# A fused recurrent attention and feed-forward kernel: the column of log w by one product, u by SyncE, the first sums of Y reordered, the decay mask on ScalarE

## The chip, the cores and the metric

One Trainium2 chip, one of its cores. TensorE (PE in the profile), VectorE (DVE), ScalarE (ACT), GpSimd (POOL) and SyncE (SP) run beside each other and wait for each other by semaphores; 16 DMA engines move data between HBM and SBUF. Products land in PSUM, which has 8 banks. The metric is the device time of one execution in microseconds, median of the runs.

## The reference

Two stages. First a recurrence for each of 4 x 8 heads over 768 steps, with a 48 x 48 state that decays by w:

```python
B, H, S, D = r.shape                       # 4, 8, 768, 48
for t in range(S):
    kt, vt, rt = (k[:, :, t].copy(), v[:, :, t].copy(), r[:, :, t].copy())
    cur = np.einsum('bhd,bhe->bhde', u[None] * kt, vt)
    y[:, :, t] = np.einsum('bhd,bhde->bhe', rt, state + cur)
    state = w[None, :, :, None] * state + np.einsum('bhd,bhe->bhde', kt, vt)
```

Then y, as x of 3072 x 384, goes through a feed-forward layer with the square of a ReLU:

```python
h = np.maximum(x @ w_in, 0.0)              # w_in 384 x 2048
return (h * h @ w_out)                     # w_out 2048 x 384
```

## The kernel before

The 768 steps of each batch are cut into 6 chunks of 128; a chunk of one batch with all 8 heads is a *unit*, 24 in all. Units 0 to 3, the first two chunks of batches 0 and 1, are handled as two *pairs* (q = 0, 1): a load of r, k or v fetches 256 steps, and partition p holds steps 2p and 2p + 1. Inside a unit the recurrence becomes matrix products. With the factors w^(t-128) and w^(127-t) (`Wt`, `Wk`, exponentials of multiples of log w, L295 and L299), r and k are scaled (`rh` L341, `kh` L338), transposed (by PE in the first units, `TR`, `TK` L365 and `T` L399; later by the DMA, `XB` L405), and multiplied with each other (`Ap` L385, `A` L412). A mask makes the product strictly causal (`Bp` L393, `Bm` L420), and the masked matrix times v gives Y (`YE` L458, `YD` L438, `Y` L482). The chunks before add rT times the state S0W (`YI` L469, `Y` L480). The state takes k times v (`UP` L492, `U` L502) and a decay mask `WLm` that holds w^128 on the blocks of the diagonal (`S0` L516, `ts` L519, `S` L522). The step's own term is a row sum of r k u (`P0` L344, `P1` L348, `du` L351) times v (`dv` L356): in the pairs PE adds it to Y by a product with the identity (L450, L429), later it is added when Y is copied to bf16 (`xs` L513; L252 on ACT and L254 on DVE are the helper `copy`).

That x is transposed (`X` L527 on PE with the copy `xTc`, later `xX` L534 by the DMA), and enters the feed-forward stage: `F1` (L543; `FA` L555 for the first columns of group 0, one unit at a time) gives hidden blocks of 128 x 512, in groups of two units; `re` (L565 on ACT, L567 on DVE) and `sq` (L572, L574) make the squared ReLU; `F2` (L583) multiplies by w_out into a PSUM bank, `os` copies it out, and `out` (L634, L636) stores it. `V` (L332) and `W` (L335) load quarters of w_in and w_out on POOL's queue, cast to bf16 on the way.

The order is written out by hand. `ORDER` (L25 to L112) is a list of steps `name.indices:engine/slots`, issued from first to last (L645 to L656): `Bp.0.1.1:D/0` is the mask of pair 0, half 1, head parity 1, on DVE, into buffer 0 of its pool. Engines are A (ACT), D (DVE), G (POOL), P (PE), S (SyncE, loads and stores). A PE step's slots are PSUM banks. Each engine runs its own steps in the order of the list, and a wait holds up everything behind it on that engine.

The head of the list, which the change touches most: `w` and `u` (L258, L261) load w and u as one row each. `lw` (L267) takes the logarithm of the w row. `bw` and `bu` (L270, L273) spread the rows over 128 partitions by a product with ones, and `ub` copies u's to SBUF. `bc` (L304) needs log w as a column, one partition for each of the 2 x 48 entries of a head pair, and gets it with eight products of 1 x 128 by 1 x 1 (four, of two passes each); `WLcol` (L310) makes w^128 of it, and `WLm` (L315) spreads that into the mask. `Z` (L615) are products of the identity with itself that nobody reads. `lp` loads the pairs (L326), `ld` the later units (L322).

DVE's order in the head is rh.1, kh.0, P0.0, rh.0, kh.1, rh.3, rh.2, kh.2, kh.3, P1.1, du.0, du.1, the masks Bp.0.1.1, Bp.0.0.1, Bp.0.1.0, Bp.0.0.0, S0.0, ts.1, Bp.1.0.1, xTc.0, Bp.1.0.0, S0.2, ts.3, du.2, re.0.6, du.3. POOL's, behind P1.0 and V.2, is dv.0, dv.1, WLm, P0.2, P1.2, P0.3, P1.3, dv.2, dv.3, W.1, rh.5, W.2, W.3, W.0. PE's is Z.8, bw, bc, bu, TR.0, TK.0, TR.1, Z.2, Ap.0.1, Ap.0.0, TK.1, UP.0, YE.0.1, Z.7, YE.0.0, Ap.1.0, YI.1, UP.1, X.0, X.1, FA.0.0.

Of the kernel before, what the change touches and what calls it, by code (L numbers as in the profile page):

```python
# [30 lines left out]
vb.3:A/2 WLm:G Z.7:P/7 vb.2:A/3 Bp.0.0.0:D/3 YE.0.0:P/2/0 Ap.1.0:P/7/3 P0.2:G/2 S0.0:D ld.v.4:S/4 P1.2:G ts.1:D/1
xs.0:A/0 YI.1:P Bp.1.0.1:D/4 UP.1:P/4/6 X.0:P/5 xs.1:A/1 xTc.0:D/3 Bp.1.0.0:D/6 S0.2:D X.1:P/2 FA.0.0:P/0/3 ts.3:D/0
xTc.1:A/3 FA.0.1:P/0/3 P0.3:G/3 P1.3:G du.2:D/2 re.0.6:D/0 F1.0.0:P/5 dv.2:G du.3:D/3 dv.3:G Wt.2:A re.0.0:A/1 W.1:G
ld.v.5:S/5 Wk.2:A F1.0.1:P/4 Ap.1.1:P/0/2 Bp.1.1.1:D/5 F1.0.2:P/7 re.0.1:A/2 F1.0.3:P/5 rh.5:G/4 re.0.7:A/3
Bp.1.1.0:D/7 YD.1:P/1/2 YI.3:P sq.0.7:A/0 re.0.3:A/4 W.2:G xs.3:D/2 xs.2:A/3 kh.4:D/5 re.0.2:A/5 ld.k.6:S/6 W.3:G
F1.0.4:P/6 X.2:P/4 X.3:P/2 xTc.3:A/0 sq.0.0:A/2 xTc.2:D/0 sq.0.1:D/1 rh.4:D/5 F1.0.5:P/5 W.0:G re.0.4:D/3 sq.0.6:A/3
re.0.5:A/2 P0.4:D/4 F1.1.4:P/1 T.4:P/0 Tc.4:D/4 F1.1.7:P/4 sq.0.5:D/4 F1.1.5:P/5 re.1.4:D/1 re.1.7:A/0 ld.r.6:S/6
sq.0.4:A/5 F1.1.1:P/0 re.1.5:D/2 re.1.1:A/3 sq.1.5:D/6 sq.0.3:D/7 F1.1.0:P/6 kh.5:D/4 F1.1.2:P/4 sq.1.1:A/8 F1.1.6:P/5
re.1.2:A/2 re.1.0:D/4 T.5:P/0 re.1.6:D/3 F2.0.2:P/4 F1.1.3:P/6 ld.r.7:S/7 Tc.5:A/5 P1.4:D du.4:D/4 sq.0.2:D/9
A.4:P/5/0 A.5:P/1/2 sq.1.6:A/10 re.1.3:A/5 sq.1.3:A/11 F2.0.1:P/4 sq.1.0:A/12 F2.0.3:P/4 vb.4:G/4 Bm.4.1:D/0  # L40
Bm.4.0:D/1 sq.1.7:A/13 P0.5:D/1 Bm.5.1:D/2 sq.1.4:A/14 F2.1.1:P/5 Bm.5.0:D/3 F2.1.2:P/5 ld.k.7:S/7 dv.4:G Y.4:P/0
P1.5:G du.5:D/0 F2.3.2:P/6 sq.1.2:A/15 ld.v.7:S/6 ld.k.9:S/0 xs.4:D/4 F2.0.0:P/4 vb.5:A/5 Y.5:P/0 dv.5:D xs.5:D/0
F2.3.0:P/6 P0.6:G/0 P1.6:G ld.v.6:S/7 F2.3.1:P/6 os.0:D/0 ld.r.9:S/0 X.4:P/0 xTc.4:D/1 U.4:P/4 F2.1.0:P/5 X.5:P/0
F2.1.3:P/5 S0.4:D xTc.5:D/1 rh.7:G/6 F1.2.0:P/4 os.1:D/1 F1.2.4:P/0 P0.7:G/2 re.2.0:D/3 out.1:S F1.2.2:P/5 kh.7:D/6
re.2.4:A/5 kh.6:G/0 F1.2.6:P/4 re.2.6:A/4 ld.r.8:S/1 vb.6:A/6 re.2.2:A/0 XB.7:S/6 rh.6:D/0 F1.2.3:P/0 F2.3.3:P/6
kh.9:D/1 re.2.3:A/1 P1.7:D XB.6:S/1 F2.2.2:P/4 os.3:D/2 F1.2.1:P/5 du.7:D/1 S.1:D ld.k.8:S/1 U.5:P/0 S0.5:D dv.7:G
U.6:P/6 re.2.1:A/2 sq.2.1:A/16 F2.2.3:P/4 ld.r.11:S/2 ts.6:D/1 F2.2.1:P/4 sq.2.3:D/17 P0.9:G/3 sq.2.0:A/18 ld.r.10:S/3
F2.2.0:P/4 sq.2.6:A/19 F1.2.7:P/0 os.2:D/3 du.6:D/2 A.7:P/5/6 A.6:P/1/2 ld.k.11:S/2 re.2.7:A/2 vb.7:G/7 F1.2.5:P/4
Bm.7.1:D/0 sq.2.2:A/20 rh.8:G/2 F2.4.0:P/0 ld.k.10:S/3 Bm.7.0:D/1 Bm.6.0:D/2 Bm.6.1:D/3 sq.2.7:A/21 rh.9:G/1 S.3:G
F2.4.1:P/0 re.2.5:D/1 ld.v.8:S/0 XB.9:S/0 P1.9:D dv.6:G out.2:S F2.4.3:P/0 rh.11:G/3 F2.5.0:P/6 ld.v.9:S/1 sq.2.4:A/22  # L50
Y.6:P/5 rh.10:G/5 ld.r.13:S/5 sq.2.5:A/23 F2.5.3:P/6 xs.6:D/1 Y.7:P/4 X.6:P/5 kh.8:G/2 F2.5.1:P/6 xs.7:D/2 P0.8:D/4
xTc.6:A/2 X.7:P/4 U.7:P/5 kh.10:G/5 F2.4.2:P/0 xTc.7:A/2 ts.7:D/0 kh.11:D/3 XB.11:S/2 vb.8:A/0 F1.3.1:P/4 os.4:A/4
S.7:D F1.3.7:P/5 re.3.1:A/3 P0.10:D/1 du.9:D/3 XB.8:S/3 U.8:P/0 F2.5.2:P/6 re.3.7:A/4 vb.9:G/1 S.6:D F1.3.3:P/4
os.5:A/5 XB.10:S/4 P1.8:D re.3.3:D/0 F1.3.4:P/5 F1.3.0:P/6 re.3.4:A/2 rh.13:D/4 ld.k.13:S/4 F1.3.2:P/3 ts.8:D/0
ld.v.11:S/2 re.3.0:A/5 sq.3.1:D/24 U.9:P/5 ld.v.10:S/3 F1.3.5:P/7 re.3.2:A/1 ts.9:D/1 sq.3.0:A/25 sq.3.3:D/26
A.11:P/1/2 A.9:P/6/4 P0.11:D/2 P1.11:G sq.3.2:A/27 F2.6.0:P/5 ld.r.12:S/4 Bm.9.1:D/2 re.3.5:A/3 F2.6.1:P/5 sq.3.7:A/5
Bm.9.0:D/3 ld.v.12:S/4 dv.9:G sq.3.5:A/7 Bm.11.1:D/5 F1.3.6:P/4 Bm.11.0:D/7 sq.3.4:A/3 du.8:D/4 kh.13:G/4 A.10:P/3/7
A.8:P/0/6 re.3.6:A/5 F2.7.0:P/2 Bm.8.0:D/0 sq.3.6:A/9 ld.k.12:S/5 ld.r.15:S/7 Y.9:P/1 vb.11:A/2 F2.7.2:P/2 Bm.8.1:D/1
dv.8:D S.9:G vb.10:A/3 ld.k.14:S/7 F2.6.3:P/5 out.4:A P1.10:G Y.8:P/4 xs.9:D/3 F2.7.3:P/2 xs.8:D/4 P0.13:G/0 X.9:P/0
Bm.10.1:D/4 X.8:P/6 F2.6.2:P/5 xTc.8:A/0 du.11:D/0 xTc.9:D/0 rh.12:G/0 Y.11:P/1 U.10:P/4 du.10:D/2 dv.10:G out.0:S  # L60
# [5 lines left out]
P0.15:G/2 sq.4.3:A/6 F1.5.2:P/4 P1.12:D re.5.7:A/1 ld.k.19:S/3 F2.9.2:P/0 re.4.0:A/4 P1.15:G sq.4.7:A/14 U.11:P/7
sq.4.1:D/10 F2.9.1:P/0 re.5.0:A/5 ld.k.21:S/2 F2.9.3:P/0 sq.5.0:A/13 ts.11:D/1 S.11:G F1.5.5:P/1 re.5.2:A/3 P1.14:D
F1.5.3:P/6 out.7:A ld.r.16:S/1 ts.12:D/0 re.5.5:D/0 sq.4.0:A/11 F1.5.6:P/7 kh.14:G/2 os.6:A/7 F2.8.2:P/4 vb.13:A/5
re.5.6:D/2 dv.13:G F2.9.0:P/0 XB.14:S/0 sq.5.6:A/15 du.12:D/3 A.13:P/2/1 sq.5.5:A/8 A.12:P/5/7 re.5.1:D/5 F2.8.1:P/4
sq.5.7:A/12 XB.15:S/6 Bm.12.0:D/2 P0.17:G/1 sq.5.2:A/16 F2.8.3:P/4 Bm.12.1:D/3 re.5.3:A/4 F2.8.0:P/4 ld.v.14:S/7  # L70
# [617 lines left out]
```

## Time and profile before

| what | value |
|---|---|
| median of 3 runs | 169.44 us (169.03 to 169.59) |
| the profiled execution | 170.19 us |
| its span, first to last instruction | 168.5 us |
| granted clock, core 0 | 1.000 |
| HBM read, written | 20.45 MB, 4.72 MB |

The busiest groups, as instructions x mean: L583 on PE 368 x 326 ns, L543 on PE 612 x 264 ns, L572 on ACT 70 x 626 ns, L565 on ACT 67 x 595 ns, L420 on DVE 40 x 681 ns. Means are from start to modelled end; matmuls overlap, so the distance from one start to the next is shorter.

How to read the rows: a row in order of time is "start us, us, engine line operation out<-in shape xcount [idle before <-what ended it]". Rows of the same line are merged, so that the second number of a row with x4 covers four instructions from the first start to the last end; consecutive instructions of one engine overlap by some 0.1 us. "SPq" and "ACTq" are the issuing of a DMA. A row of the chain of waits is "start, us, what": the chain that ended last, traced back. A row by stretches gives, for each engine, busy us and the number of instructions, then the granted clock, the share of the 16 DMA engines' time and GB/s; the share can pass 1 as packets overlap.

### The profile page before, as it was taken

The page shows a single profiled execution, that of the slowest core. Times are in us where ns is not written, and L with a number is a line of the kernel's source. Part 1 is how long each engine was busy: PE and PEld are TensorE (multiplying, and loading weights), DVE is VectorE, ACT ScalarE, POOL GpSimd, SP SyncE. Part 2 cuts the span into 40 slices and gives each one's busy share as a digit, 9 for nine tenths or more (in the row PEclk, how much of TensorE's full clock was granted, in tenths as well). Part 3 has the DMA queues.
Part 4 walks back from the last instruction along what each step waited for, and adds up shares of the span by engine and source line. Part 5 has one row for each costly group of instructions (what it writes and reads, how often), then busy time and mean ns, then how long its engine had stood idle before and what let it go on. Part 6 is the DMA issues. An engine that isn't in the chain of part 4 may idle for free.

```text
span 168.5 us, 4507 instructions
## 1 busy us (share of the span) xinstructions
PE 161.8 (96%) x1778; PEld 122.4 (73%) x1778; DVE 134.3 (80%) x253; ACT 101.4 (60%) x189; POOL 100.5 (60%) x125
## 2 busy tenths in 40 slices
PE   4999999899999999999999999999999999999993
PEld 1686888568766867788766888666887666898762
DVE  5689979987999979989897969998878965955400
ACT  4687697831772697349782469941298492254731
POOL 6779781248399218995999797599536660300000
PEclk9999999999999999999999999999999999999999
DMA  5999999979999799999999999995879931320032
GB/s 131 321 236 193 196 150 215 205 141 205 150 180 197 154 204 211 202 192 200 191 204 139 220 227 220 174 199 135 162 163 130 267 86 24 108 83 0 2 142 95
DMA packets 97785, 28.02 MB, mean 166 GB/s; under 512 B 92530, under 2 KB 97524, under 8 KB 97764
## 3 DMA queue, kind: packets, MB, share of 16 engines
q1 hardware_dynamic: 93872, 22.42, 67.6%
q0 software_dynamic: 3008, 4.13, 12.8%
q10 hardware_dynamic: 884, 1.18, 2.2%
q8 instruction: 14, 0.23, 0.6%
q14 instruction: 7, 0.06, 0.1%
HBM read 20.45 MB, written 4.72 MB: 149 GB/s over the span
## 4 chain that ended last, share of the span: by engine, by line
PE 63%; DMA 16%; DVE 7%; POOL 6%; issue 4%; SPq 3%; ACT 0%; POOLq 0%
PE bank L583 28%; PE bank L543 26%; DMA W<-in_moe_w_out_dram 6%; DMA ldk<-in_k_dram 3%; DMA ldr<-in_r_dram 2%; DMA xT<-xs 2%; PE bank L482 2%; DMA rkT<-rk 2%; SPq L326 2%; PE bank L412 2%; DVE Bm L420 2%; PE bank L480 2%; PE bank L597 2%; POOL dv L356 1%; POOL P L348 1%
## 5 line engine op out<-in xcount | busy, mean ns | idle before, releaser
L583 PE MATMUL bank<-W,hq 128*128 128x384 bf16 x368 | 68.7, 326 | 0.6 <-DMA W<-in_moe_w_out_dram 0.4
L543 PE MATMUL bank<-xT,W 128*128 128x256 bf16 (+1 forms) x612 | 68.6, 264 | 0.2 <-DMA xT<-xs 0.2
L565 ACT ACTIVATE hr<-bank 128x512 bf16<-128x512 f32 x67 | 38.9, 595 | 37.6 <-PE bank L543 33.6
L543 PEld LDWEIGHTS <-W 128*128 128x128 bf16 x612 | 54.7, 98 | 8.8 <-DMA xT<-xs 0.6
L583 PEld LDWEIGHTS <-hq 128*128 128x128 bf16 x368 | 33.9, 98 | 19.3 <-issue 0.7
L572 ACT ACTIVATE hq<-hr 128x512 bf16<-128x512 bf16 x70 | 40.9, 626 | 4.6 <-DVE hr L567 4.1
L420 DVE TENSOR_TENSOR Bm<-bank,maskJT 128x512 bf16<-128x512 f32 x40 | 25.5, 681 | 3.2 <-PE bank L412 3.1
L567 DVE TENSOR_SCALAR hr<-bank 128x512 bf16<-128x512 f32 x29 | 19.6, 684 | 7.0 <-PE bank L543 4.9
L356 POOL TENSOR_TENSOR dv<-ldv,du 128x384 f32<-128x384 f32 (+1 forms) x18 | 15.9, 891 | 11.5 <-DVE du L351 8.2
L348 POOL TENSOR_TENSOR P<-P,ub 128x384 f32<-128x384 f32 x15 | 15.9, 1062 | 11.2 <-DVE P L344 10.8
L344 POOL TENSOR_TENSOR P<-ldr,ldk 128x384 f32<-128x384 f32 x13 | 13.7, 1054 | 4.7 <-DMA ldr<-in_r_dram 3.4
L341 POOL TENSOR_TENSOR rk<-ldr,Wt 128x384 bf16<-128x384 f32 x15 | 16.5, 1105 | 0.0
L574 DVE TENSOR_TENSOR hq<-hr 128x512 bf16<-128x512 bf16 x26 | 13.3, 523 | 2.1 <-ACT hr L565 1.9
L338 POOL TENSOR_TENSOR rk<-ldk,Wk 128x384 bf16<-128x384 f32 x12 | 12.6, 1055 | 2.6 <-DMA ldk<-in_k_dram 2.6
L513 DVE TENSOR_TENSOR xs<-bank,dv 128x384 bf16<-128x384 f32 x20 | 11.0, 552 | 2.6 <-PE bank L482 1.1
L351 DVE TENSOR_REDUCE du<-P 128x8 f32<-128x384 f32 x24 | 12.8, 542 | 0.0
L522 POOL TENSOR_TENSOR S0W<-ts,WLm 128x384 bf16<-128x384 f32 x10 | 10.3, 1032 | 1.5 <-DVE ts L519 1.5
L254 DVE COPY os<-bank 128x384 f32<-128x384 f32 x11 | 6.0, 550 | 6.2 <-PE bank L583 6.1
L519 DVE TENSOR_TENSOR ts<-bank,S0W 128x384 f32<-128x384 f32 x16 | 8.8, 550 | 2.1 <-PE bank L502 1.1
L482 PE MATMUL bank<-vb,Bm 128*128 128x48 bf16 x160 | 9.5, 183 | 0.0
L252 ACT COPY os<-bank 128x384 f32<-128x384 f32 (+2 forms) x14 | 6.3, 460 | 4.5 <-PE bank L583 2.5
L254 POOL CAST vb<-ldv 128x384 bf16<-128x384 f32 x10 | 5.6, 564 | 5.7 <-DMA ldv<-in_v_dram 5.7
(87 smaller groups left out, 173.4 us busy)
## 6 DMA issues: line engine op xcount, KB each, us to landing
ldr<-in_r_dram SPq DMA_DIRECT2D x20, 192.0 KB, 3.8
ldk<-in_k_dram SPq DMA_DIRECT2D x20, 192.0 KB, 4.1
ldv<-in_v_dram SPq DMA_DIRECT2D x20, 192.0 KB, 3.5
out_dram<-os SPq DMA_DIRECT2D x9, 192.0 KB, 2.4
W<-in_moe_w_in_dram POOLq DMA_DIRECT2D x4, 384.0 KB, 9.2
W<-in_moe_w_out_dram POOLq DMA_DIRECT2D x4, 384.0 KB, 8.5
...
```

The costliest lines, as they stand in the source:

```text
L341: e.tensor_mul(rk[slot[f"rk{i}"]][:, 0, :, 0:D], loaded("r", i), Do.factor("t", i % 2 if i < PAIRED else 2))
L344: e.tensor_mul(P0b[slot[f"P{i}"]], loaded("r", i), loaded("k", i))
L348: e.tensor_mul(t, t, bank("bu")[:, 0 : H * D].rearrange("p (h d) -> p h d", h=H) if i in EARLY_U else ub)
L356: e.tensor_mul(dv_of(i) if i < PAIRED else dvb[slot[f"dv{i}"]], loaded("v", i), t)
L420: e.tensor_mul(Bmb[slot[f"Bm{i}{h}"]], heads(bank(f"bA{i}{h}"), 128), mask_b)
L482: e.matmul(y[:, hc, D * h : D * (h + 1)], m[h][:, hc, :], vb[:, 2 * hc + h, :], start=(c == 0), stop=True, skip_group_check=True,)
L543: e.matmul(hp[:, fi, :], W1[f // 4][:, c, 256 * (f // 2 % 2) : 256 * (f // 2 % 2 + 1)].rearrange("p (m j) -> p j m", j=2)[:, f % 2, :], xt ...
L565: e.activation(hr, hp, AF.Relu)
L567: e.tensor_scalar_max(hr, hp, 0.0)
L572: e.activation(hq, hr, AF.Square)
L574: e.tensor_mul(hq, hr, hr)
L583: e.matmul(bank(f"bO{i}")[:, 0:d_model], hqb[slot[f"hq{g},{f // m}"]][:, at : at + L], W2[q][:, f % 4, :], start=(seen[i] == 1 and f % 4 = ...
```

## The change

- **bc.** `w4` (on ACT's queue, where u was) loads w as 4 partitions of 2 x 48; `l4` (ACT) takes its logarithm into a zeroed 4 x 2 x 64 tile; `bc` is one product of that tile with a 4 x 4 identity, and stands behind TK.0 on PE instead of between bw and bu.
- **u** is loaded by SyncE, behind the first r and ahead of the first k.
- **YE.** The four products with dv come behind the last products of YE.0.0, not ahead of those of YE.0.1; the first product of each bank opens it (start), all others add. Ap.1.0 goes ahead of YE.0.0.
- **WLm** goes from POOL to ACT, between RC.1 and KC.1; WLcol from between the factors to behind KC.0.
- **Z.2 and Z.7** are gone. Two small DVE steps (zeroing of the tile, the 4 x 4 identity) are added at the start.
- **DVE's head** becomes rh.1, rh.0, kh.0, kh.1, P0.0, rh.3, rh.2, P1.1, du.1, kh.2, kh.3, du.0, the masks; re.0.6 goes to ACT.
- **POOL's head:** dv.1 ahead of dv.0; w_out's quarters in the order W.2, W.1, rh.5, W.3, W.0.
- **Later:** sq.0.2 ahead of P1.4 (DVE); F1.2.5 ahead of A.7; A.9 ahead of A.11; U.10 from behind Y.11 to ahead of X.9; F2.19.0 and Y.22 ahead of F1.10.2 (all PE); P1.9 (unit 9's product with u) from ahead of xs.6 to behind xs.7; xTc.9 ahead of du.11 (DVE); out.14 from SyncE to POOL, out.12 earlier on POOL. Some 40 steps get other PSUM banks.

```diff
-w:A mP.0:G mP.1:G lp.r.0:S/0 lp.k.0:S/0 tab:A lw:A Z.8:P/0 bw:P/1 lp.r.1:S/1 lp.v.0:S/0 mJ:G u:A lp.k.1:S/1 Wt.1:A/2
-lp.v.1:S/1 bc:P/3 P0.1:G/0 Wk.0:A/4 rh.1:D/0 ld.r.5:S/4 Wt.0:A/5 bu:P/6 kh.0:D/1 V.3:G WLcol:A P0.0:D/1 Wk.1:A/7
...
+w:A mP.0:G mP.1:G lp.r.0:S/0 u:S lp.k.0:S/0 tab:A lw:A Z.8:P/0 w4:A bw:P/1 lp.r.1:S/1 lp.v.0:S/0 mJ:G lp.k.1:S/1
+bu:P/6 Wt.1:A/2 lp.v.1:S/1 Wt.0:A/5 rh.1:D/0 P0.1:G/0 Wk.0:A/4 rh.0:D/1 Wk.1:A/7 ld.r.5:S/4 kh.0:D/1 V.3:G kh.1:D/0
+ub:A l4:A TR.0:P/0 P0.0:D/1 V.0:G ld.k.4:S/4 RC.0:A/0 TK.0:P/3 rh.3:D/2 rh.2:D/3 V.1:G P1.1:D du.1:D/1 bc:P/6 TR.1:P/2
+KC.1:A/3 vb.3:A/2 Ap.1.0:P/6/0 vb.2:A/3 Bp.0.0.0:D/3 YE.0.0:P/5/3 P0.2:G/2 S0.0:D ld.v.4:S/4 P1.2:G ts.1:D/1 xs.0:A/0
...
+    w4t = const.tile([HP, 2, D], FP32, name="w4")
+    l4t = const.tile([HP, 2, 64], FP32, name="l4")
+    eye4 = const.tile([HP, HP], FP32, name="eye4")
...
+    nc.vector.memset(l4t, 0.0)
...
+    nc.vector.tensor_copy(eye4, identity[0:HP, 0:HP])
...
+        def w4(e):
+            e.dma_start(out=w4t, in_=w.rearrange("(a b) d -> a b d", b=2))
+
+        def l4(e):
+            e.activation(l4t[:, :, 0:D], w4t, AF.Ln)
+
         def bc(e):
-
-            for hc in range(HP):
-                e.matmul(
-                    bank("bc")[:, hc : hc + 1], pair(lrow.rearrange("p (o a) b -> p o a b", o=1), 0, hc), ones[:, 0:1],
-                    start=True, stop=True, skip_group_check=True,
-                )
+            e.matmul(bank("bc")[:, 0:HP], l4t.rearrange("p a b -> p (a b)"), eye4, start=True, stop=True)
...
-                e.tensor_copy(
-                    WLm[64 * h : 64 * h + D, :, D * h : D * (h + 1)],
+                copy(
+                    e, WLm[64 * h : 64 * h + D, :, D * h : D * (h + 1)],
...
         def YE(e, q, h):
             y = [heads(bank(f"bY{2 * q + x}"), 2 * D) for x in range(2)]
-            if h:
-                for a in range(2):
-                    for x in range(2):
-                        e.matmul(
-                            y[x][Do.half(a)], identity[Do.half(x), Do.half(x)],
-                            dv_of(2 * q + a)[Do.half(x)].rearrange("p (a e) d -> p a (e d)", e=2),
-                            start=True, stop=False, skip_group_check=True,
-                        )
             for hc in range(HP):
...
+                            start=(h == 1 and hc == 0 and a == 0), stop=(a == 1 and h == 1), skip_group_check=True,
+                        )
+            if h == 0:
+                for a in range(2):
+                    for x in range(2):
+                        e.matmul(
+                            y[x][Do.half(a)], identity[Do.half(x), Do.half(x)],
+                            dv_of(2 * q + a)[Do.half(x)].rearrange("p (a e) d -> p a (e d)", e=2),
                             start=False, stop=True, skip_group_check=True,
                         )
```

More of the change, by code (lines that the diff above doesn't have):

```diff
@@ L31 @@
[L31 to L60, printed above, removed]
@@ L66 @@
[L66 to L70, printed above, removed]
@@ L103 @@
+F2.18.1:P/6 Bm.22.0:D/7 F2.18.3:P/6 Bm.22.1:D/5 F2.18.0:P/6 F2.19.0:P/3 Y.22:P/4 F1.10.2:P/2 re.10.2:D/3 F1.10.0:P/0
+xs.22:D/2 Bm.23.1:D/6 xX.22:S/0 F1.10.1:P/1 os.18:D/2 F1.10.5:P/5 re.10.0:D/2 out.18:G F1.10.3:P/2 re.10.5:D/5
 Y.23:P/4 sq.10.5:D/22 F2.19.2:P/3 xs.23:D/3 re.10.3:A/4 sq.10.3:A/23 xX.23:S/1 sq.10.2:A/0 F1.11.1:P/7 out.17:G
```

107 lines of the change are left out of this document (69 added, 38 removed).

## The prediction, as it was put on record

> **What bounds the kernel now.** I read first the busy shares of the page and the busy time by stretches, then the chain of waits up to 45 us, then the order in time of PE, DVE, POOL, ACT and SyncE up to 36 us, and at last PE's few gaps after that. In each fence rows of one view stand in order of time, with others between them left out.
>
> ```profile
> PE 161.8 (96%) x1778; PEld 122.4 (73%) x1778; DVE 134.3 (80%) x253; ACT 101.4 (60%) x189; POOL 100.5 (60%) x125
> ...
> 20.60:24.00 3.40, 3.40 (x66) 2.73 (x64) 2.29 (x7) 3.08 (x7) 3.38 (x6) 1.00 0.86 129
> 24.00:33.00 9.00, 8.43 (x89) 6.60 (x88) 8.77 (x18) 7.23 (x13) 1.95 (x3) 1.00 1.16 205
> ...
> 32.90 2.11 PE L583 MATMUL bank<-W,hq 128*128 128x384 bf16 x12 [0.43 <-DMA W<-in_moe_w_out_dram]
> ```
>
> PE is busy for 96% of the span, and its feed-forward products cannot be had for less. So the time is the moment at which they begin, plus their sum, plus the gaps. What can be gained lies before 16.63 us, where the first of them starts (below), and in the gaps, of which that at 32.90 is the largest. The DMA engines (the share ahead of the GB/s) are full from 24 to 33 us, at 1.16, and less so in the stretch before, at 0.86.
>
> What sets 16.63? Rows of DVE, of PE and of ACT:
>
> ```profile
> 9.61 1.02 DVE L338 TENSOR_TENSOR rk<-ldk,bank 128x384 bf16<-128x384 f32 x2 [0.75 <-DMA ldk<-in_k_dram]
> 10.54 0.55 DVE L348 TENSOR_TENSOR P<-P,ub 128x384 f32<-128x384 f32 x1
> 11.01 1.00 DVE L351 TENSOR_REDUCE du<-P 128x8 f32<-128x384 f32 x2
> 11.94 2.47 DVE L393 TENSOR_TENSOR Bm<-bank,maskP 128x512 bf16<-128x512 f32 x4
> ...
> 7.81 2.74 PE L365 MATMUL bank<-identity,rk 128*128 128x128 bf16 x24
> 13.15 0.51 PE L450 MATMUL bank<-dv,identity 64*64 64x384 bf16 x4
> 15.39 0.51 PE L492 MATMUL bank<-vb,rk 64*128 64x96 bf16 x16
> 15.84 0.53 PE L527 MATMUL bank<-identity,xs 128*128 128x128 bf16 x6
> 16.63 1.50 PE L555 MATMUL bank<-xT,W 128*128 128x128 bf16 x24 [0.26 <-DVE xT L254]
> ...
> 14.87 1.10 ACT L252 CAST xs<-bank 128x384 bf16<-128x384 f32 x2 [0.22 <-PE bank L458]
> ```
>
> DVE is done with rh.3 and rh.2 at 8.86, waits 0.75 for the second k load, which lands at 9.59 (chain row below), and then runs without a pause: kh.2, kh.3, P1.1, du.0, du.1 and four masks Bp, until 14.41. Behind the last mask come YE.0.0, the copy xs.0 (14.87), the transposes X (15.84, behind UP.1 at 15.39), the copy to xT and the first feed-forward product (16.63).
>
> **The change part by part.**
>
> *DVE's order in the head.* P1.1 and du.1 move ahead of kh.2, into the wait for k. They cost 11.01 - 10.54 = 0.47 and (11.94 - 11.01) / 2 = 0.46, and can start when the DVE pipeline takes the next one, near 8.79: du.1 lasts until 9.72. kh.2 then starts at 9.72 instead of 9.61, with kh.3, du.0 and the first mask behind it: that mask moves by 0.11 - 0.93 = -0.82, from 11.94 to 11.12. P1.1 needs the broadcast u by 8.79:
>
> ```profile
> 4.68 1.70 PE L304 MATMUL bank<-ones,lrow 1*128 1x1 f32 x8
> 6.25 1.62 PE L273 MATMUL bank<-urow,ones 1*128 1x384 f32 x2
> ...
> 2.29 0.23 ACTq L261 DMA_DIRECT2D urow<-in_u_dram  x1
> 6.42 0.17 ACT L310 ACTIVATE wcol<-bank 128x4 f32<-128x4 f32 x1
> 7.91 0.48 ACT L252 COPY ub<-bank 128x384 f32<-128x384 f32 x1 [0.87 <-PE bank L273]
> ```
>
> *One product for the column of log w.* The eight small products (6.25 - 4.68 = 1.57 of PE) leave the way, so bu can start at 4.68 and end near 6.3; the copy ub (0.48), behind the four factors on ACT, is done near 7.3, 1.5 ahead of need. So u may land as late as 6 without a loss. The transposes TR.0 start when rh.0 is done, now second instead of fourth on DVE, near 6.6 instead of 7.81, and RC.0, KC.0 and the products Ap come earlier with them; the masks wait for DVE, not for these. The new product with two passes costs some 2 x 1.70/8 = 0.43 behind TK.0, where PE waits for rh.2 anyway. If l4 were late, TR.1 and Ap would queue behind it; it is about as small as L310 (0.17), and its load goes out where u's did, 5 us before. RC.0, KC.0 and the casts of v stand behind l4 on ACT and have those 1.2 us to give.
>
> *u on SyncE.* One more issue ahead of k.0. It took 0.23 on ACT; here it delays every load behind it by 0 (if the DMA engines set the pace) to 0.28 (that and the step):
>
> ```profile
> 0.81 0.46 SPq L326 DMA_DIRECT2D ldr<-in_r_dram  x1
> 1.94 1.10 SPq L326 DMA_DIRECT2D ldr<-in_r_dram  x1
> 4.28 5.31 DMA ldk<-in_k_dram
> ```
>
> The third issue takes 1.10 where the first of the same size took 0.46: the queue is full by then, and the pace is not that of issuing. I take 0; with kh.2 at 9.72 the first 0.11 of a delay is free anyhow, which leaves 0.17 for the range.
>
> *Y of pair 0.* YE.0.1 no longer waits for dv; the four products with dv (13.15 to the next at 13.60, 0.45) come behind YE.0.0 instead. So xs.0 gains only 0.82 - 0.45 = 0.37 and starts near 14.5. That doesn't bind: X.0 waited for UP.1 until 15.84, half a microsecond after xs.0 was done (14.87 + 0.48 = 15.35). With YE done near 14.5, YI.1, UP.1 (0.45 to X.0) and xs.0 all end near 15.05, and the first feed-forward product comes near 15.88: **-0.75**. Z.2 and Z.7, products that feed nothing, go too.
>
> *The decay mask on ACT.* It leaves POOL (0.74 below) and stands on ACT ahead of KC.1 and the casts of v.2 and v.3. KC.1 waits for TK.1, so for kh.3, until about 12; RC.1 is done near 11.5. Two copies of at most 0.37 end at 12.2 at the latest. A push of 0.2 on KC.1 would pass to Ap.1.0 and Bp.1.0, which are wanted from 14.6 on and have over 1 us. I take 0.
>
> ```profile
> 18.14 0.54 DVE L351 TENSOR_REDUCE du<-P 128x8 f32<-128x384 f32 x1
> ...
> 13.22 0.74 POOL L315 COPY WLm<-wcol 48x192 f32<-48x192 f32 x2
> 19.83 0.83 POOL L356 TENSOR_TENSOR dv<-ldv,du 128x384 bf16<-128x384 f32 x1 [0.23 <-DVE du L351]
> 21.38 1.01 POOL L341 TENSOR_TENSOR rk<-ldr,Wt 128x384 bf16<-128x384 f32 x1
> 22.33 2.19 POOL L335 DMA_DIRECT2D W<-in_moe_w_out_dram  x3
> ...
> 23.08 9.77 DMA W<-in_moe_w_out_dram
> ```
>
> With the mask off POOL, dv.2 and dv.3 wait for DVE alone: du.2 comes at 18.14 - 0.75 = 17.4, du.3 right behind it since re.0.6 goes to ACT (idle there), and two times 0.83 from 17.95 on end at 19.6 instead of 20.66. So the issues of w_out come about 1.05 earlier. W.2, wanted first, goes first; W.3, whose landing at 32.85 ends the gap at 32.90, is issued from 22.0 instead of 23.08. The transfers start where the DMA engines had room (0.86). Bounds for its landing: unmoved, which leaves PE at 32.90; or 1.05 and more earlier (rh.5, 1.01, no longer parts the first two), and then PE gains its 0.75 and the gap, 1.18 in all. I take **-0.8 to -1.05** there.
>
> *Past 34 us.* What is left of that must pass one spot, where DVE runs without a pause from the landing of r.13 to xs.9 and xs.8, and PE waits for those:
>
> ```profile
> 38.68 0.97 SPq L322 DMA_DIRECT2D ldr<-in_r_dram  x1
> 40.44 1.19 SPq L634 DMA_DIRECT2D out_dram<-os  x2
> 55.88 4.05 DMA ldr<-in_r_dram
> 59.95 0.56 DVE L341 TENSOR_TENSOR rk<-ldr,Wt 128x384 bf16<-128x384 f32 x1 [0.87 <-DMA ldr<-in_r_dram]
> 67.26 1.01 DVE L513 TENSOR_TENSOR xs<-bank,dv 128x384 bf16<-128x384 f32 x2
> 69.68 0.17 PE bank L502 x4
> ```
>
> r.13 is issued in an almost unbroken row of SyncE steps that starts at 40.44 with out.1, which waits for a copy that PE drives; SyncE is idle from 39.65 to 40.44. So that row, and DVE's with it, can start **0.8** earlier even if no load before it does. I carry -0.8. At this spot U.10 (0.17) moves ahead of X.9 into PE's wait: **-0.17**. The swap of A.9 and A.11, F1.2.5 ahead of A.7, and P1.9 (unit 9's product with u) behind xs.6 and xs.7 fill gaps ahead of this spot, so they count 0. Other bank numbers, dv.1 ahead of dv.0, out.14 and out.12 on POOL: 0, since the trace has PE waiting for no bank; a bank that comes free late would cost at most the copy that frees it, 0.5 to 0.7.
>
> *The end.*
>
> ```profile
> 139.34 2.12 PE L583 MATMUL bank<-W,hq 128*128 128x384 bf16 x12
> 141.71 0.83 PE L543 MATMUL bank<-xT,W 128*128 128x256 bf16 x6 [0.25 <-DMA xT<-xs]
> 143.56 0.65 PE bank L583 x4
> 142.65 0.69 DVE L567 TENSOR_SCALAR hr<-bank 128x512 bf16<-128x512 f32 x1 [1.55 <-PE bank L543]
> ```
>
> Twelve products at 0.65 per four end at 141.30; the next starts at 141.71, so 0.41 is lost. F2.19.0 (0.65) and Y.22 now lie in that wait. But on DVE re.10.2 (142.65) still stands ahead of xs.22 and gets its product later, so unit 22's transpose may come up to 0.45 later. Between 0 and -0.41 I take **-0.25**.
>
> **Sum:** -0.8 - 0.17 - 0.25 = -1.22. The profiled execution took 170.19 (its span 168.5 and 1.7 around it), so 168.97 by its own time; the median of the runs shown is 169.44, 0.75 less, which gives **168.2**.
>
> **The rivals.**
>
> *A: the loads hold it.* If r.13 lands when it does now, DVE's run and PE behind 67.9 stay where they are; only -0.17 - 0.25 = -0.4 is left: 169.0. For it: the share of 1.16 up to 33 us. Against: SyncE's idle 0.79.
>
> *B: PE stays at half rate for longer; slower than before.* Twenty-four products of 128 columns take 2.74 us from 7.81 on and 1.50 from 16.63 on. The PEclk row shows nothing of it. The slow ones still run here:
>
> ```profile
> 11.86 0.92 PE L365 MATMUL bank<-identity,rk 128*128 128x128 bf16 x8
> ```
>
> So PE reaches its full rate only after nearly unbroken work from 7.81 to 12.78, 5.0 us. The change takes Z.2, Z.7 and eight products out. If the waits between the masks now break the run, the count starts anew at 15.88, half rate lasts until 20.9 and costs 2.5: 169.44 - 1.22 + 2.5 = 170.7. It decides from a switch at 15.88 + 2 x 1.22 = 18.3 on. Against it: TR.0 to UP.0 is about as dense as before, 1 us earlier (6.6 to 12.4). The Trainium skill, "TensorE: Matmul & The Clock Gate", section "Part 1: The HAM clock gate", says that the clock is halved until a free-running window of about 3.4 us has been busy. By that rule, an estimate, a first busy window that ends by 15.9 costs nothing, and one that ends at 19.3 costs 1.7 and gives 169.9. The trace agrees that the rate doubles late; where the window stands, no run here shows.
>
> *C: all of it comes through.* PE 1.18 early behind 32.9, the loads follow, the end gives 0.41: -1.18 - 0.17 - 0.41 = -1.76, 167.7.
>
> *D: the change doesn't do all it says in the head*, since u, the masks on ACT or the dv products push xs. Half of the 0.8 is left: 168.6, within the forecast's own range.
>
> **How the numbers follow.** Forecast with D 0.54 (167.9 to 168.9), A 0.22 (168.8 to 169.4), B 0.14 (169.5 to 170.8), C 0.10 (167.3 to 167.9). The range of 167.4 to 169.8 leaves out most of B and the edge of C. A measurement of this kernel can tell 0.3%, 0.5 us, from no change: faster is below 168.93, slower above 169.95. Faster: 0.51 + 0.10 + a third of A = 0.68; slower: most of B, 0.11; same: 0.21.
>
> **What would show it.** Right: the first mask on DVE at 11.1, the first feed-forward product at 15.9, W.3 landed by 32.1 with PE's gap there no longer than 0.4, r.13 at 59.1, xs.8 by 67.5, no wait of F1 for xT near 140. Wrong: P1.1 waiting for ub, or k.1 landing past 9.72; 128 columns still at 0.11 us behind 15.9; r.13 still at 59.9; a new wait for a bank.

## The result and the profile after

The change made the kernel slower: 171.63 us against 168.94 us, ratio 1.0131 (95% interval 1.0082 to 1.0181); in a second set, beside other runs, 1.0073 (1.0034 to 1.0111). The forecast was 168.2 us, range 167.4 to 169.8. Times are medians of all executions, while ratios compare undisturbed executions only, on both sides: of the runs below, e11 lost half of its executions to that, and e18's profiled one ran at a mean granted clock of 0.58, so that only its times are used.

The profiled execution took 171.94 us, span 170.2; the one before 170.19 and 168.5. The last product starts 1.75 later (167.16 instead of 165.41), as the whole time. Busy shares of the page after, which hardly move:

```profile
PE 162.9 (96%) x1766; PEld 122.5 (72%) x1766; DVE 134.7 (79%) x254; ACT 102.3 (60%) x193; POOL 99.8 (59%) x124
```

The head after, in order of time, SyncE's issues, POOL and DVE:

```profile
1.32 0.46 SPq L266 DMA_DIRECT2D urow<-in_u_dram  x1
...
6.83 1.00 POOL L350 TENSOR_TENSOR P<-ldr,ldk 128x384 f32<-128x384 f32 x1 [2.47 <-DMA ldk<-in_k_dram]
7.79 2.49 POOL L338 DMA_DIRECT2D W<-in_moe_w_in_dram  x3
...
6.79 1.02 DVE L344 TENSOR_TENSOR rk<-ldk,bank 128x384 bf16<-128x384 f32 x2 [0.25 <-DMA ldk<-in_k_dram]
9.12 0.71 DVE L354 TENSOR_TENSOR P<-P,ub 128x384 f32<-128x384 f32 x1
10.40 1.02 DVE L344 TENSOR_TENSOR rk<-ldk,bank 128x384 bf16<-128x384 f32 x2
11.81 2.47 DVE L399 TENSOR_TENSOR Bm<-bank,maskP 128x512 bf16<-128x512 f32 x4
```

k.0 lands at 6.69 (5.45 before). DVE waits 0.25 for it and POOL 2.47, so that the loads of w_in go out at 7.79 instead of 6.53. P1.1 starts 0.33 later than forecast (9.12, not 8.79) and takes 0.71 instead of 0.55 (to the start of the next one 0.74, forecast 0.47), k.1 lands at 10.38 (9.59 before), and the first mask comes at 11.81: of the forecast 0.82, 0.13 is left.

PE after, in order of time:

```profile
15.68 0.82 PE L498 MATMUL bank<-vb,rk 64*128 64x96 bf16 x16
16.43 0.82 PE L533 MATMUL bank<-identity,xs 128*128 128x128 bf16 x6
...
17.38 2.33 PE L561 MATMUL bank<-xT,W 128*128 128x128 bf16 x24
...
32.98 2.83 PE L589 MATMUL bank<-W,hq 128*128 128x384 bf16 x16
...
37.99 0.37 PE L488 MATMUL bank<-vb,Bm 128*128 128x48 bf16 x8 [0.67 <-DVE xs L519]
...
58.49 0.81 PE L549 MATMUL bank<-xT,W 128*128 128x256 bf16 x6 [0.45 <-DVE ts L525]
...
141.33 2.77 PE L589 MATMUL bank<-W,hq 128*128 128x384 bf16 x16
```

FA starts 0.75 later (16.63 before) and its 24 products take 2.33 instead of 1.50: until 19.15 they run at half rate. The gap at 32.9 is gone, as forecast: W.3 lands at 31.99, and its four products start at 33.65 inside the row at 32.98, 0.75 later than before only because PE comes later. Two waits are new, before Y.5 (37.99) and in F1.3 (58.49). From one start to the next, less the columns, they cost 0.83 and 0.61. The gap of 0.41 near 141 is gone, as forecast (F2.19.0 is part of the row at 141.33), but (below) other executions without the change lack it too.

POOL after, and the longest piece of the chain of waits:

```profile
21.08 1.48 POOL L341 DMA_DIRECT2D W<-in_moe_w_out_dram  x2
22.57 1.02 POOL L347 TENSOR_TENSOR rk<-ldr,Wt 128x384 bf16<-128x384 f32 x1
23.52 1.48 POOL L341 DMA_DIRECT2D W<-in_moe_w_out_dram  x2
34.46 0.67 POOL L259 CAST vb<-ldv 128x384 bf16<-128x384 f32 x1 [9.46 <-DMA ldv<-in_v_dram]
```

```profile
21.09 13.31 DMA ldv<-in_v_dram
```

The issues of w_out (W.2, W.1, W.3, W.0) begin at 21.08, not at the forecast 19.55, and W.3 goes out at 23.52, not 22.0; before, the first went out at 20.60 and W.3 at 23.08. The load of v.4, issued with W.2, takes 13.31 us; before it landed at 27.08, 6.58 after its issue:

```profile
27.14 0.50 POOL L254 CAST vb<-ldv 128x384 bf16<-128x384 f32 x1 [2.63 <-DMA ldv<-in_v_dram]
```

### The profile page after: what moved, and what is told of

Same layout as the page of the kernel before. It is cut to its first block, busy times and chain, and to the rows that moved or that the text cites. A ratio compares the mean times of both kernels' runs of the same rounds, so it can differ in the third digit from the quotient of the medians.

```text
span 170.2 us, 4485 instructions
## 1 busy us (share of the span) xinstructions
PE 162.9 (96%) x1766; PEld 122.5 (72%) x1766; DVE 134.7 (79%) x254; ACT 102.3 (60%) x193; POOL 99.8 (59%) x124
## 3 DMA queue, kind: packets, MB, share of 16 engines
q0 software_dynamic: 3072, 4.33, 13.1%
## 4 chain that ended last, share of the span: by engine, by line
PE 73%; SPq 12%; DMA 8%; DVE 2%; issue 2%; POOL 1%; ACT 0%; DVEq 0%
PE bank L589 32%; PE bank L549 31%; DMA ldv<-in_v_dram 8%; SPq L328 8%; SPq L332 4%; PE bank L418 3%; PE bank L488 2%; PE bank L486 2%; PE bank L508 2%; PE bank L603 2%; PE bank L533 1%; DVE xs L519 1%; DVE dv L362 1%; POOL P L354 1%; POOL dv L362 0%
## 5 line engine op out<-in xcount | busy, mean ns | idle before, releaser
L571 ACT ACTIVATE hr<-bank 128x512 bf16<-128x512 f32 x68 | 39.4, 594 | 38.2 <-PE bank L549 35.7
L573 DVE TENSOR_SCALAR hr<-bank 128x512 bf16<-128x512 f32 x28 | 18.7, 684 | 6.5 <-PE bank L549 4.6
L350 POOL TENSOR_TENSOR P<-ldr,ldk 128x384 f32<-128x384 f32 x13 | 13.3, 1020 | 4.7 <-DMA ldk<-in_k_dram 2.5
L347 POOL TENSOR_TENSOR rk<-ldr,Wt 128x384 bf16<-128x384 f32 x15 | 15.6, 1042 | 0.7 <-DMA ldr<-in_r_dram 0.7
L580 DVE TENSOR_TENSOR hq<-hr 128x512 bf16<-128x512 bf16 x26 | 13.8, 545 | 2.2 <-ACT hr L571 2.0
L259 POOL CAST vb<-ldv 128x384 bf16<-128x384 f32 x10 | 6.3, 631 | 10.9 <-DMA ldv<-in_v_dram 10.9
L488 PEld LDWEIGHTS <-Bm 128*128 128x128 bf16 x160 | 8.2, 96 | 2.0 <-DVE xs L519 1.1
```

The costliest lines, as they stand in the source:

```text
L347: e.tensor_mul(rk[slot[f"rk{i}"]][:, 0, :, 0:D], loaded("r", i), Do.factor("t", i % 2 if i < PAIRED else 2))
L488: e.matmul(y[:, hc, D * h : D * (h + 1)], m[h][:, hc, :], vb[:, 2 * hc + h, :], start=(c == 0), stop=True, skip_group_check=True,)
L571: e.activation(hr, hp, AF.Relu)
L573: e.tensor_scalar_max(hr, hp, 0.0)
L580: e.tensor_mul(hq, hr, hr)
```

## The experiments

Four theories. **Q**: u in SyncE's queue delays the loads behind it. **H** (rival B of the prediction): PE's half rate lasts longer. **W**: the loads of w_out keep v.4 from the DMA engines. **B** (not the prediction's B): P1.9 behind xs.7 delays ts.7 and with it a bank. Each ratio is to the kernel before, run on the same chip in the same set. H is read from the trace's records of the granted clock: full rate begins at 12.52 us before and at 19.15 after. Ahead of that the trace has no record; there products of 128 columns start 0.107 us apart, behind it 0.056. Behind each expectation stand the ratio with its 95% interval and then times in us of the profiled execution; "FA 16.88 with 1.50" is the start of FA's 24 products and what they take. In the edits, "..." stands for steps left out.

**e1_u_act**: the changed kernel, u on ACT.

```diff
-w:A mP.0:G mP.1:G lp.r.0:S/0 u:S lp.k.0:S/0 tab:A lw:A Z.8:P/0 w4:A bw:P/1 ...
+w:A mP.0:G mP.1:G lp.r.0:S/0 lp.k.0:S/0 tab:A lw:A Z.8:P/0 u:A w4:A bw:P/1 ...
```

> The changed kernel with u back on ACT's queue, ahead of w4. Theory Q (u's small load, put between the first r and the first k, holds SyncE's queue for over 1 us): k.0 lands near 5.5 instead of 6.69, k.1 near 9.6 instead of 10.38, the first mask on DVE starts near 11.1 instead of 11.81, and the time falls by 0.5 to 1.0 against the changed kernel. Theory H (PE stays at half rate until far behind the first feed-forward product, since its head has pauses): the loads land earlier, but 128-column products at 16 us still take 107 ns, and the time stays within 0.4 of the changed kernel's 171.6.

Ratio 1.0056 (1.0009 to 1.0103). k.0 lands at 5.46, the first mask comes at 11.39, FA 16.88 with 1.50, full rate at 15.94. The loads are as Q expects; the ratio is below the changed kernel's 1.0131, but not clear of the 1.0073 of the second set. The waits before Y.5 (0.70) and in F1.3 (0.61) stay.

**e2_fill**: the changed kernel with two groups of products that feed nothing.

```diff
-bu:P/6 Wt.1:A/2 ...
+bu:P/6 Z.4:P/0 Wt.1:A/2 ...
-... Ap.0.1:P/0/5 ...
+... Z.2:P/6 Ap.0.1:P/0/5 ...
```

> The changed kernel, u still on SyncE, with two fillers on PE: four identity products' worth (512 columns) ahead of TR.0 and 2 x 128 columns ahead of Ap.0.1, where the kernel before had its own. Theory H: the full PE rate comes by 16 instead of 19.15, the 24 products of FA take 1.5 instead of 2.33, and the time falls by 0.7 to 1.2 from 171.6. Theory Q alone: k.0 still lands at 6.7, FA starts near 17, and the time stays within 0.4 of the changed kernel's.

1.0066 (1.0026 to 1.0107), under the 1.0131 of the changed kernel in one other set and level with its 1.0073 in the second. Full rate begins at 18.80 in this trace, FA 16.96 with 2.36, a miss for H's switch. It stays ambiguous until e12 and e11.

**e3_before_u_sync**: the kernel before with u on SyncE behind lp.r.0.

```diff
-... lp.r.0:S/0 lp.k.0:S/0 ... mJ:G u:A lp.k.1:S/1 ...
+... lp.r.0:S/0 u:S lp.k.0:S/0 ... mJ:G lp.k.1:S/1 ...
```

> The kernel before with one edit: u loaded by SyncE between the first r and the first k. Theory Q: k.0 lands near 6.7 instead of 5.45 and k.1 near 10.4 instead of 9.59, kh.2 waits for it, and the time rises by 0.6 to 1.0 (169.6 to 170.0). Theory H alone: the loads shift by at most 0.3 and the time by at most 0.3.

1.0039 (0.9995 to 1.0082); k.0 at 6.05, first mask 12.37, FA 17.07, full rate at 11.21. So in this trace FA comes 0.44 later than in that of before, and H does not come with it; the interval of the time reaches down to no loss.

**e4_before_no_z**: the kernel before without Z.2 and Z.7.

```diff
-... Z.2:P/6 Ap.0.1:P/7/5 ... Z.7:P/7 vb.2:A/3 ...
+... Ap.0.1:P/7/5 ... vb.2:A/3 ...
```

> The kernel before with one edit: the fillers Z.2 and Z.7 are taken out of PE's order. Theory H: the full PE rate comes one window or more later than 12.5, in this profile or in part of the runs, and the time rises by 0.3 to 1.2 with a wider spread. Theory Q alone: nothing changes, within 0.3.

1.0040 (0.9994 to 1.0086), full rate at 11.80, FA 16.31: in this trace the rate doubles as early without Z.2 and Z.7.

**e5_u_act_fill**: e1 and e2 together.

> The changed kernel with the load of u on ACT (ahead of that of w by pairs) and with two groups of products that feed nothing put into PE's waits, one ahead of TR.0 and one ahead of the first Ap. H (the half rate lasts longer because PE's head is too thin): PE's clock record switches to full by 13 us and the 24 products of FA take 1.5 us; FA starts near 16.5; 0.4 to 0.8 faster than the kernel with u on ACT alone (170.38), so 169.6 to 170.0. Q (only the queue of SyncE costs): no faster than 170.4, and the switch stays near 16 or later. W and B (w_out's transfers starve ld.v.4; P1.9 delays ts.7) expect their gaps here too: 0.6 to 0.8 at 36 to 37 us and 0.5 to 0.6 at 56.

0.9988 (0.9947 to 1.0029), full rate at 14.93 (by 13 was expected), FA 16.68 with 1.50. v.4 landed at 27.54 without rh.5 between, and no wait at 36: against W as it was stated. B's 0.61 is there (ahead of 55.84).

**e6_u_act_rh5**: e1 with rh.5 between the first two loads of w_out.

```diff
-... W.1:G rh.5:G/4 W.3:G W.0:G ...
+... rh.5:G/4 W.1:G W.3:G W.0:G ...
```

> The changed kernel with u on ACT and with rh.5 between the first and the second load of w_out on POOL, as in the kernel before. W (the loads of w_out, issued back to back, keep ld.v.4 from the DMA engines): ld.v.4 lands at 26 to 27.5 us instead of 32.85, and PE's gap before Y.5 near 36 us (0.70 with u on ACT alone) is under 0.2; 0.4 to 0.7 faster than 170.38, so 169.7 to 170.0. The rival to W, that ld.v.4 is late because SyncE issues it late or POOL's vb.4 stands behind other work: the gap stays. The landing of W.3 may go back to 32.5 or later; then 0.2 to 0.4 of PE's wait at 32.9 comes back and the total moves less.

0.9987 (0.9950 to 1.0025); v.4 at 25.91, no wait before Y.5. As W expects, but v.4 is also issued 0.74 ahead of W.2 here; e13 decides.

**e7_u_act_p19**: e1 with P1.9 ahead of xs.6.

```diff
-... xs.6:D/1 Y.7:P/4 ... xs.7:D/2 P1.9:D P0.8:D/4 ...
+... P1.9:D xs.6:D/1 Y.7:P/4 ... xs.7:D/2 P0.8:D/4 ...
```

> The changed kernel with u on ACT and with P1.9 ahead of xs.6 and xs.7 on DVE, as in the kernel before. B (P1.9 behind xs.7 delays ts.7, on which the bank of F1.3.7 waits): PE's stall of 0.5 to 0.6 before F1.3.7 near 56 us is gone, and PE's waits near 60 and 68 us grow back by 0.2 to 0.5 in sum, since unit 9 comes later on DVE; so the total is within 0.4 of 170.38. The rival, that the stall comes from ts.7's own product and not from P1.9: the stall stays.

1.0034 (1.0005 to 1.0063). The wait in F1.3 is gone, so B holds; PE runs through F1.3 in one row:

```profile
56.31 2.78 PE L549 MATMUL bank<-xT,W 128*128 128x256 bf16 x24
```

**e8_all**: u on ACT right behind w, the fillers of e2, rh.5 and P1.9 back.

```diff
-w:A mP.0:G mP.1:G lp.r.0:S/0 u:S lp.k.0:S/0 ...
+w:A u:A mP.0:G mP.1:G lp.r.0:S/0 lp.k.0:S/0 ...
```

> All three undone together and the head filled: the load of u on ACT right behind that of w, two groups of products that feed nothing in PE's head, rh.5 between the first two loads of w_out, P1.9 ahead of xs.6. What is left of the change: DVE's order in the head, one product for the column of log w, the products with dv behind YE.0.0, the mask on ACT, the order of the loads of w_out, the tail. If Q, H, W and B together are the cause, the head's gain of 0.5 to 0.75 comes through: FA at 16.3 or earlier with 1.5 us, no stall over 0.5 at 36 or 56 us, and the time is 168.3 to 169.0, at most equal to the kernel before (169.2) and likely 0.2 to 0.8 faster. If it is still slower than 169.7, a cause is missing from the list.

1.0029 (0.9993 to 1.0064), a miss: full rate at 17.73, FA at 17.93. The issue of u stands ahead of the logarithm of w, which bw now awaits for longer (0.24 after), and DVE's head is pushed by 0.26 with it:

```profile
3.50 1.64 PE L275 MATMUL bank<-lrow,ones 1*128 1x384 f32 x2 [0.49 <-ACT lrow L272]
```

P1.1 took 1.42 there beside POOL's P1.0 (9.05 to 10.47; POOL 9.04 to 10.04).

**e12_after_again** and **e11_after_dense**: the changed kernel once more, and with four single products that feed nothing.

```diff
+... Z.4:P/0 Wt.1:A/2 ... Z.4:P/2 TR.1:P/2 ... Z.4:P/5 Ap.0.1:P/0/5 ... Z.4:P/7 TK.1:P/6 ...
```

> The changed kernel once more, beside the three others of this set. H (PE's rate doubles at the end of the first 3.41 us window, counted from a start that differs from execution to execution, in which the matmuls of the trace at half rate, each weighted with the share of the 128x128 array that it fills, give about 2.54 us or more): the switch falls anywhere between 14.6 and 21, on average at 18.5, and the time between 170 and 172, about 1.3% over the kernel before. Every window that ends at the switch holds 2.5 us or more of such work and every earlier one less. Against H: a switch at the same place as in the first trace (19.15) with another density, or one below 14.

> The changed kernel with nothing else than four single products that feed nothing (512 columns, 0.43 us each at half rate) in PE's head: ahead of TR.0, of TR.1, of the first Ap and of TK.1. u stays on SyncE, w_out and P1.9 stay as changed. H: the windows between 9 and 14 us pass 2.54 us in every phase, the switch comes at or before 14, FA's 24 products take 1.5 us instead of 2.3, and the kernel gains 0.7 to 1.1 on the changed one of the same chip, less what the added products push in the head (0 to 0.4). Rival (half rate costs nothing, the loss is all in the gaps behind 34 us): no faster, or up to 0.5 slower.

e12 1.0073 (1.0034 to 1.0111), e11 1.0018 (0.9972 to 1.0065): 0.55%, 0.9 us, by fillers alone, as H expects. The intervals overlap, and in the two profiled executions the switch comes alike (15.40 and 15.36; for e11, at or before 14 was expected, a miss), so the traces of this pair do not show the gain. The waits before Y.5 (0.83) and in F1.3 (0.61) are in both.

What shows H is e12 beside the first trace of the same kernel (171.94; 170.42 here). PE of e12:

```profile
15.66 0.51 PE L498 MATMUL bank<-vb,rk 64*128 64x96 bf16 x16
16.10 0.64 PE L533 MATMUL bank<-identity,xs 128*128 128x128 bf16 x6
16.89 1.50 PE L561 MATMUL bank<-xT,W 128*128 128x128 bf16 x24
```

The first mask comes 0.14 later here (11.95 against 11.81), and the same products start alike at 15.66 and 15.68. But full rate begins at 15.40 instead of 19.15, so FA starts 0.49 earlier and takes 0.83 less.

**e9_best**: e5 with rh.5 and P1.9 back. **e10_p11_back**: e9 with P1.1 and du.1 behind kh.3, as they were (du.1 now ahead of du.0).

```diff
-... P1.1:D du.1:D/1 bc:P/6 ... kh.2:D/3 kh.3:D/2 Z.2:P/6 ...
+... bc:P/6 ... kh.2:D/3 kh.3:D/2 P1.1:D du.1:D/1 Z.2:P/6 ...
```

> Q, H, W and B undone together as in e8_all, but with the load of u on ACT behind the logarithm of w, not ahead of it (in e8_all it pushed that logarithm by 0.26 and the whole head with it). All four named causes out: FA at 16.3 to 16.7 with 1.5 us, ld.v.4 landed by 28.5, no stall over 0.4 at 36 or 56 us; 168.4 to 169.0 where the kernel before has 169.4, so 0.2 to 0.6% faster. If it is no faster than the kernel before, the gain that was forecast for the head is not there even without the four.

> As e9_best, but P1.1 and du.1 on DVE stand again behind kh.3, where they stood before the change. The forecast's first step (0.82 for P1.1 and du.1 in the wait for k): this kernel loses 0.3 to 0.8 against e9_best at the first mask on DVE and at FA. Rival (k.1 lands at 9.1 once u is off SyncE and earlier loads follow on, and P1.1 takes 0.71 instead of 0.47 beside POOL's P1.0): P1.1 is back at 0.47 to 0.55 here, the first mask comes within 0.2 of e9_best's, and so does the time.

0.9983 (0.9948 to 1.0019) and 0.9982 (0.9942 to 1.0022): back at the kernel before, not below it. DVE of e9, then of e10:

```profile
8.79 0.71 DVE L354 TENSOR_TENSOR P<-P,ub 128x384 f32<-128x384 f32 x1
10.01 1.01 DVE L344 TENSOR_TENSOR rk<-ldk,bank 128x384 bf16<-128x384 f32 x2
11.59 1.89 DVE L399 TENSOR_TENSOR Bm<-bank,maskP 128x512 bf16<-128x512 f32 x3
```

```profile
9.59 1.02 DVE L344 TENSOR_TENSOR rk<-ldk,bank 128x384 bf16<-128x384 f32 x2 [0.72 <-DMA ldk<-in_k_dram]
10.53 0.55 DVE L354 TENSOR_TENSOR P<-P,ub 128x384 f32<-128x384 f32 x1
12.04 1.28 DVE L399 TENSOR_TENSOR Bm<-bank,maskP 128x512 bf16<-128x512 f32 x2
```

The new order brings the first mask 0.45 earlier and FA 0.20 (16.48 against 16.68), and the time not at all.

**e13_after_rh5**: the changed kernel, u on SyncE, with rh.5 between as in e6.

> The changed kernel, u on SyncE, with nothing else than rh.5 back between the first and the second load of w_out on POOL. W as it now stands: where SyncE issues ld.v.4 less than 0.3 us ahead of W.2 or behind it, and the loads of w_out follow each other without rh.5, its data land only behind the third of them (32.9 to 34.4 in the five traces where that is so), and PE waits 0.7 to 0.8 before Y.5. With rh.5 between, ld.v.4 lands by 28 and that wait is under 0.2, at the same place of v.4 against W.2; 0.4 to 0.8 faster than the changed kernel (171.07 in the last set). Rival (v.4 is late because its issue is late): the landing stays at 33 or later and so does the wait.

1.0049 (1.0003 to 1.0095). POOL, then PE before Y.5:

```profile
19.87 0.76 POOL L341 DMA_DIRECT2D W<-in_moe_w_out_dram  x1
20.65 1.01 POOL L347 TENSOR_TENSOR rk<-ldr,Wt 128x384 bf16<-128x384 f32 x1
21.60 2.19 POOL L341 DMA_DIRECT2D W<-in_moe_w_out_dram  x3
30.50 0.50 POOL L259 CAST vb<-ldv 128x384 bf16<-128x384 f32 x1 [6.71 <-DMA ldv<-in_v_dram]
```

```profile
35.18 0.36 PE L488 MATMUL bank<-vb,Bm 128*128 128x48 bf16 x8
36.68 0.33 PE L533 MATMUL bank<-identity,xs 128*128 128x128 bf16 x3
```

v.4 is issued 0.92 *behind* W.2 and lands at 30.44, not by 28 as expected, but 3 us before the 33.4 to 34.4 of the changed kernel, and PE no longer waits. So W in its final form needs both: v.4 issued behind W.2 or shortly ahead of it (0.12 ahead is late in e1, 0.31 ahead is not in e5), and no break in the loads of w_out.

**e14_old_head**: the code of before and its order up to FA.0.1; from P0.3 on the order of the change, with the edits of e6 and e7.

> The kernel before up to FA (its code and its order, u on ACT where it was), then the order of the changed one, with rh.5 and P1.9 back in their places. So the parts of the change behind 17 us alone: the order of the loads of w_out, U.10, F1.2.5, the swap of A.9 and A.11, the tail, the bank numbers. If these carry a gain of their own (the gap at 32.9, those at 48, 60 and 68, and 0.25 of the tail, of which the forecast counted 0.3 to 0.7), it is 0.2 to 0.5% faster than the kernel before, PE's gaps behind 17 us sum to 3.6 to 3.9 as in e9_best, where the kernel before has 5.2, and FA starts at 16.3 to 17.0. If the gaps of the kernel before were accidents of one execution, the time is that of the kernel before within 0.2%.

1.0040 (1.0009 to 1.0071): the parts behind 17 us gain nothing, and by the interval they cost up to 0.7%; PE has a gap of 0.79 ahead of 150.27, at an xT from the DMA, in the new tail.

**e15_dv_first**: e9 with the code of YE from before, the products with dv first.

```diff
+            if h:
+                for a in range(2):
...
-            if h == 0:
-                for a in range(2):
```

> As e9_best, but the four products with dv open the bank of Y again, ahead of YE.0.1, as in the kernel before. If they lengthen the chain from the last mask to FA when they stand behind YE.0.0 (0.29 us at full rate, 0.45 to 0.54 at half rate), FA comes 0.2 to 0.5 earlier than in e9_best (16.48), at 16.0 to 16.3, and the time is 0.1 to 0.4 lower (169.33 there). Rival (the chain waits for something else between, the copy rT of RC.1 and KC.1 or UP.1): FA stays within 0.1 of 16.48. If dv comes late on POOL, YE.0.1 waits and nothing is gained.

0.9929 (0.9899 to 0.9960), 0.7% faster than the kernel before, although its profile has a gap of 1.27 ahead of 108.78 (ts late on DVE, behind the wait for a v load). PE of e15, then of e9:

```profile
16.19 1.50 PE L561 MATMUL bank<-xT,W 128*128 128x128 bf16 x24
```

```profile
16.48 1.50 PE L561 MATMUL bank<-xT,W 128*128 128x128 bf16 x24
```

FA is 0.29 earlier, as expected; the rest of the 0.9 us between the two kernels is not in these rows.

**e16_after_dv_first**, **e17_before_dv_last** and **e18_dv_first_no_fill**: the changed kernel with the old YE; the kernel before with the new YE; e15 without the fillers. (The edit of e16 is the diff of e15, that of e17 its reverse; e18 takes e2's diff back.)

> The changed kernel with nothing else than the four products with dv opening the bank of Y again, as in the kernel before. Y (with dv behind YE.0.0 the last mask is followed by 0.3 us of PE work more at full rate and 0.45 to 0.55 at half rate): FA comes 0.3 to 0.5 earlier than in the changed kernel (16.88 to 17.38 in its two traces), and PE's head is denser around 13, so that the full rate comes earlier on average; together 0.5 to 1.2 faster than the changed kernel, ratio to the kernel before 1.000 to 1.006 where the changed one has 1.007 to 1.013. PE's waits at 36 and 56 us stay. Rival (e15_dv_first was fast for another reason): FA moves by less than 0.15 and the ratio stays at 1.007 or more.

> The kernel before with nothing else than the products with dv behind YE.0.0, as the change has them. Y: YE.0.1 no longer waits for dv, but FA comes 0.2 to 0.4 later than 16.63, and the time is 0.1 to 0.3% over the kernel before. The forecast of the change (the products with dv only take from the slack of xs.0, X.0 waits for UP.1 anyway): FA within 0.1 of 16.63 and the time within 0.1%. Rival: without the wait for dv the masks and YE end earlier, and FA gains 0.1 or more.

> As e15_dv_first without the two groups of products that feed nothing. H: the windows between 10.5 and 13 lose 0.1 to 0.5 us of filled work, so in a part of the executions the full rate comes one window later, behind 14; 0 to 0.4 slower than e15_dv_first (ratio 0.9929). If the fillers only cost, 0.1 to 0.2 faster.

e16 1.0103 (1.0049 to 1.0158), a miss, with FA at 17.38 and full rate at 18.36; e17 1.0022 (0.9985 to 1.0058) with FA at 16.43; e18 0.9984 (0.9946 to 1.0021), further from e15 than the 0.4 us that were expected. So the place of the products with dv alone decides nothing; only together with the dense head and the loads of e9 does it go with a gain. Why e15 beats both e9 and e18 by 0.9 us (the intervals just touch) stays open.

## Why the prediction was wrong, step by step

- **u on SyncE, priced at 0 with 0.28 as the far end: this step failed first.** "the pace is not that of issuing" was read from one full-queue row. k.0 landed 1.24 later in this trace and 0.36 to 0.90 later in the other six with u on SyncE, and w_in's loads left 1.26 later. The first mask lost 0.42 of its gain (11.81 against 11.39 in e1), but that is not so in each execution: with u on SyncE it comes at 11.81 and 11.95 where k.1 lands at 10.38 and 10.53 (after, e12), and at 11.38 to 11.51 where k.1 lands by 10.08 (e2, e11, e13, e16).
- **Rival B, given 0.14, cost most in the profiled execution.** The switch at 19.15 lies behind the 18.3 from which it was to decide, and FA ran at half rate; in e12 the same kernel switches at 15.40, so it comes true in a part of the executions only. Between the two, FA starts 0.49 later and takes 0.83 more. Over all traces, the way from the first mask to FA is 4.55 to 4.89 us in the eight where full rate begins by 13.1, 4.77 to 5.67 in six where it begins at 14.4 to 15.4, and 5.49 to 5.87 in the five where it begins from 15.9 on. The argument against B failed: "TR.0 to UP.0 is about as dense as before". Weighted as below, the two windows of 3.41 us ahead of the one that ends at the switch hold 2.15 and 2.43 us of work in the trace after (8.8 to 12.2 and 12.2 to 15.6), where that of before from 9.0 to 12.4 holds 2.77. What thins PE's work (the later k, bc between the transposes, the products taken out) was not tried piece by piece. That fillers alone took 0.9 us off (e11 against e12) supports it, with overlapping intervals. B's own picture, a count of 5.0 us that starts anew, is not what the traces show (last section).
- **DVE's order: mis-sized.** 0.82 forecast, 0.55 with u off SyncE (e1), 0.13 as changed. P1.1 takes 0.71 in its new place, 0.55 in the old. And the 11.94 from which the 0.82 was counted was late itself: the old order puts the first mask at 11.56 to 11.61 in e4, e14 and e17, where k.1 lands at 9.18 to 9.26 instead of 9.59; the new order with u on ACT puts it at 11.39 to 11.64 (e1, e5, e6, e7, e9, e15). Where the mask came earlier, FA followed by less than half (e9 against e10), the time not at all. FA, forecast at 15.88, starts at 16.17 at the earliest in all traces (e13).
- **w_out's order: right in the landing, wrong in the way there and in what it set off.** W.3 landed at 31.99 and the gap at 32.9 went, though W.3 was issued 0.44 later than before and not 1.05 earlier: dv.2 and dv.3 waited for du.2, which came at 18.90, not at 17.4. Why it landed earlier all the same stays open. That v.4 stands in the same engines' way was not in the list of costs; PE paid 0.83 for it at 37.
- **P1.9 and the bank, priced at 0: 0.61.** The rule "a bank that comes free late would cost at most the copy that frees it, 0.5 to 0.7" had the right size; the trace of before could not show the wait since P1.9 stood elsewhere.
- **The gaps that were to be won were those of one execution.** The profiled run, 170.19, lay above the median by 0.75, and the prediction subtracted that at the end, but counted its gaps as if each run had them. The gap of 0.41 at 141 is in none of e3, e4 and e17, whose order there is the same; that of 0.59 at 32 is 0.42, nothing and nothing in them. So the -0.25 of the tail and a part of the -0.8 were there to be had in some executions only; e14's time, no lower than that of before, agrees. The 0.75 that DVE waits for k in the trace before, into which P1.1 was to move, is of this kind too.
- **The products with dv, the mask on ACT:** e17 bears out that the first cost nothing measurable in the kernel before; the second wasn't tried alone.

By the runs, then: H is shown by two executions of one kernel and by the order of all traces. W and B are shown by their waits in every trace with and without; their worth in the total is within the intervals. Q is shown in the landing of k.0; in the time, u on ACT is lower in each of three pairs that differ in u alone (e1 against the changed kernel by 0.75% or, in the second set, 0.17%; e5 against e2 by 0.78%; e6 against e13 by 0.62%), always across sets and with intervals that overlap (those of e5 and e2 by 0.03% only). That a late k thins PE's head, so that Q and H overlap, is argued, not shown. With these edits e5, e6, e9 and e10 are back at the kernel before; how the total loss divides among the four stays open.
